# Attention scores from float32 keys and queries on eight 64x32 tiles, with three shared PSUM banks

## The chip, the cores and the metric

The kernel runs on one core of a Trainium2 chip. TensorE (PE) multiplies, VectorE (DVE), ScalarE (ACT) and GpSimd (POOL) work on elements, SyncE (SP) issues all transfers. SBUF has 128 partitions; PSUM, where PE writes, has eight banks of 512 float32 a partition. The metric is the device time of one execution in microseconds (us).

## The reference

Block-sparse attention with 4 batches, 8 heads, 768 positions and head size 64, followed by a feed-forward layer (FFN) with a rational function:

```python
    scores = scale * np.matmul(q, k.transpose(0, 1, 3, 2))      # scale = 1/8
    # mask: blocks of 32; a query block sees its neighbours (+-1), block 0,
    # block 23 and three sampled blocks; query blocks 0 and 23 see all
    scores = np.where(mask, scores, -1000000000.0)
    scores = scores - np.max(scores, axis=-1, keepdims=True)
    attn = np.exp(scores)
    attn = attn / (np.sum(attn, axis=-1, keepdims=True) + 1e-09)
    x = np.matmul(attn, v)                                      # then to [3072, 512]
    h = x @ w_in                                                # [3072, 2048]
    P = a[0] + a[1] * h + a[2] * h**2 + a[3] * h**3
    Q = 1.0 + np.abs(b[0]) * np.abs(h) + np.abs(b[1]) * h**2
    out = (P / (Q + 1e-06)) @ w_out                             # [3072, 512]
```

Inputs are float32, but for w_in and w_out (float64) and the numbers of the sampled blocks (integers).

## The kernel before

Attention is cut into *parts*: one query block (32 positions) of all eight heads against 8 key blocks (256 positions). An inner query block is one part (three neighbours, three sampled blocks, two edge blocks), blocks 0 and 23 take three parts each, so there are 28 parts a batch and 112 in all. The FFN is cut into 12 chunks of 256 tokens with 8 *units* each, 96 in all; a unit is 256 tokens by 256 of the 2048 inner columns.

*A part* runs so: scores on PE (`scores`, L872) into a PSUM tile `sp`, row maxima on DVE with the mask added (`maxima`, L882), the exponent on ACT (L897), four transposes on PE (L940) into `pt`, a copy to SBUF as `pT` on ACT (L147, inside the helper `times`), the product with the values on PE (L997) into `av`, and a division on DVE (L1024). Four query blocks together are transposed (L1034) into an `sp` tile and copied out as two float16 halves, `xh` on ACT and `xl` on DVE (L1046).

*The scores* use float16 pairs. A key or query tile is first scaled by a power of two, found from a bound: ACT sums absolute values (`bound`, L384), PE transposes the sums (L335), DVE takes the largest and makes the power (`scales`, L340 to L352). Then the tile is split into a high half (`high`, POOL) and a low half (`low`, DVE, L378), the halves are transposed on PE in eight matmuls (L660 keys, L733 queries), and copied to SBUF. The 128 partitions hold 64 elements high and 64 low. For queries a second copy `qc` with the halves exchanged is made by two DMAs (`swap`, L741); keys times `qa` and keys times `qc` add up to the full product. A part takes 16 matmuls of 128x32 tiles, four at a time in different columns, into one PSUM bank. The product of the two scales is undone in the exponent by a tensor `cq` (L721 to L727). For batches 1 to 3 the keys are loaded twice, once for the bound and once for the split (L580 and L532), and written to DRAM as `ks`, from where each part loads its 8 blocks into `kall` or `xkg`. For batch 0 they stay in `kall`, and POOL copies the sampled blocks to `kx` (L825).

*A unit* has two groups of 12 float16 matmuls (L1099 to L1101) into `ph`, five ACT and seven DVE instructions of 512 columns, and two groups of six matmuls (L1155 to L1157) into `acc`. The float64 weights arrive as 32 pieces through two load buffers `wl` and are decoded mainly by DVE (L434, L437, L440) during the first 250 us.

*The order* of all engines is made by the list planner `issue`: each `Op` has an engine, a price in ns, a priority, predecessors, and `Slot`s of `Ring`s, which stand for buffers. The planner takes the operation that can begin first by its prices. Where PE would wait before 80 us of planned time it puts in filling matmuls (`fill`, L159), which write to the accumulator's bank. PSUM rings: two banks `ph`, two `sp` (scores, transposed keys, queries, outputs and scales), one `pt`, and fixed banks for `av` and `acc`. Each engine then runs its list strictly in order.

## Time and profile before

| | us |
|---|---|
| median of 3 runs | 906.2 (902.2 to 910.01) |
| span of the profiled execution, first to last instruction | 897.2 |
| PE busy (share of the span) | 824.4 (92%) |
| DVE busy | 760.5 (85%) |
| ACT busy | 652.7 (73%) |
| POOL busy | 152.1 (17%) |
| chain that ended last: PE, DVE, DMA, ACT | 66%, 12%, 9%, 7% |

The span is the profiled execution's own time as far as the page gives it; 9.0 us lie between it and the median of the runs. Busy times overlap: an engine at 92% is the bound only where it is at 100%, so the busy times are read by stretch. PE's instructions are recorded with their latency: a record of 0.28 us follows the one before by 0.11. A share of the chain says which engine's work stood last at each moment.

### The profile page before, as it was taken

To read this page: it belongs to the slowest core of one execution; us is meant where nothing else is said; L and a number is where in the kernel's file an instruction comes from. 1 tells how busy PE (TensorE), PEld (TensorE's weight loads), DVE (VectorE), ACT (ScalarE), POOL (GpSimd) and SP (SyncE) were. 2 spreads that over 40 slices of the span, in tenths; PEclk is the share of its full clock that TensorE was granted. 3 is DMA by queue.
4 is the path that set the end of the run, shared out by engine and by line. 5 is a ranking of instruction groups with operands and counts; after the bars stand their busy time and mean duration, and the time that the engine had idled before them with its cause. 6 is when DMAs were issued, how large, how long until landed. Compare 5 with 4: busy or idle time off the path is not lost.

```text
span 897.2 us, 27426 instructions
## 1 busy us (share of the span) xinstructions
PE 824.4 (92%) x10310; PEld 640.1 (71%) x10310; DVE 760.5 (85%) x2042; ACT 652.7 (73%) x1380; POOL 152.1 (17%) x185
## 2 busy tenths in 40 slices
PE   6879868576899999989999999989999999999997
PEld 3446546465778787778888777778888877788885
DVE  4778978999998889879888788979888988788885
ACT  5587756677876878697778777788758687767563
POOL 2563743635310000110000000200000000000000
PEclk8989988698899999999999999999999999999999
DMA  8889686467966987688666986787756566740000
GB/s 222 186 186 233 177 175 165 113 166 202 237 162 168 239 227 172 176 207 196 165 150 184 250 204 157 168 208 197 155 148 176 145 160 169 172 110 25 1 24 24
DMA packets 238484, 148.04 MB, mean 165 GB/s; under 512 B 16016, under 2 KB 222736, under 8 KB 238352
## 3 DMA queue, kind: packets, MB, share of 16 engines
q1 hardware_dynamic: 238352, 146.29, 65.3%
q8 instruction: 82, 1.34, 0.7%
q14 instruction: 50, 0.41, 0.2%
HBM read 128.92 MB, written 11.01 MB: 156 GB/s over the span
## 4 chain that ended last, share of the span: by engine, by line
PE 66%; DVE 12%; DMA 9%; ACT 7%; SPq 3%; issue 2%; POOL 0%; ACTq 0%; POOLq 0%; DVEq 0%
PE acc L1155 8%; PE ph L1099 8%; PE acc L1157 8%; PE acc L1156 8%; PE ph L1101 7%; PE ph L1100 7%; PE av L997 6%; PE pt L940 5%; PE sp L872 4%; DMA wl<-in_moe_w_in_dram 2%; ACT pr L897 2%; PE acc L159 1%; DMA ld<-in_k_dram 1%; DVE pr L882 1%; DMA ks<-kt 1%
## 5 line engine op out<-in xcount | busy, mean ns | idle before, releaser
L1099 PE MATMUL ph<-xh,wi 128*128 128x256 f16 x768 | 210.9, 275 | 2.6 <-DVE tt L1116 2.6
L1101 PE MATMUL ph<-xh,wi 128*128 128x256 f16 x768 | 209.8, 273 | 0.0
L1100 PE MATMUL ph<-xl,wi 128*128 128x256 f16 x768 | 209.7, 273 | 0.0
L1155 PE MATMUL acc<-wo_h,gh 128*128 128x512 f32 x384 | 164.5, 428 | 5.0 <-ACT ld L147 4.9
L1157 PE MATMUL acc<-wo_h,gl 128*128 128x512 f32 x384 | 155.1, 404 | 7.3 <-DVE gl L1144 4.9
L897 ACT ACTIVATE pr<-pr,st,cq 128x256 f32<-128x256 f32 x224 | 132.3, 595 | 38.1 <-DVE st L908 35.1
L1156 PE MATMUL acc<-wo_l,gh 128*128 128x512 f32 x384 | 154.8, 403 | 1.6 <-POOL wo_l L451 1.6
L1106 ACT ACTIVATE sq<-ph,fc 128x512 f32<-128x512 f32 x96 | 65.6, 684 | 70.6 <-PE ph L1101 70.6
L151 POOL TENSOR_SCALAR hlq<-ldq,scq 128x512 f16<-128x512 f32 x24 | 24.8, 1032 | 452.1 <-DVE scq L352 235.4
L1123 DVE SCALAR_TENSOR_TENSOR ab<-sq,absb,ab 128x512 f32<-128x512 f32 x96 | 72.0, 750 | 34.4 <-ACT ab L1120 34.0
L1099 PEld LDWEIGHTS <-wi 128*128 128x128 f16 x768 | 75.2, 98 | 28.5 <-issue 16.2
L1157 PEld LDWEIGHTS acc<-wo_h,gl 128*128 128x128 f32 x384 | 74.1, 193 | 27.5 <-DVE gl L1144 7.6
L882 DVE CUSTOM_DVE_ANT_1 pr<-sp,bias 128x256 f32<-128x256 f32 x224 | 84.7, 418 | 6.9 <-PE sp L872 6.5
L1155 PEld LDWEIGHTS acc<-wo_h,gh 128*128 128x128 f32 x384 | 74.3, 194 | 21.4 <-ACT ld L147 5.2
L997 PE MATMUL av<-vg,pT 128*32 128x64 f32 x3584 | 74.4, 224 | 13.5 <-DMA vg<-in_v_dram 9.1
L1156 PEld LDWEIGHTS acc<-wo_l,gh 128*128 128x128 f32 x384 | 74.3, 193 | 14.8 <-POOL wo_l L451 2.1
L997 PEld LDWEIGHTS av<-vg,pT 128*32 128x32 f32 x3584 | 56.5, 111 | 39.6 <-issue 21.2
L940 PE MATMUL pt<-ident,pr 128*128 128x128 f32 x448 | 78.4, 296 | 5.0 <-ACT pr L897 2.3
L1100 PEld LDWEIGHTS <-wi 128*128 128x128 f16 x768 | 75.4, 98 | 10.2 <-issue 2.7
L1101 PEld LDWEIGHTS <-wi 128*128 128x128 f16 x768 | 75.2, 98 | 9.0 <-issue 0.2
L1134 DVE SCALAR_TENSOR_TENSOR gh<-tt,par,rr 128x512 fp32r<-128x512 f32 x96 | 73.9, 770 | 8.2 <-PE acc L1156 7.7
L147 ACT ACTIVATE pT<-pt 128x512 f32<-128x512 f32 x112 | 66.6, 594 | 18.1 <-PE pt L940 17.3
(141 smaller groups left out, 1697.1 us busy)
## 6 DMA issues: line engine op xcount, KB each, us to landing
vg<-in_v_dram SPq DMA_DIRECT2D x312, 64.0 KB, 3.4
vg<-in_v_dram SPq DMA_DIRECT2D x88, 192.0 KB, 3.9
vg<-in_v_dram SPq DMA_DIRECT2D x24, 512.0 KB, 4.7
kall<-ks SPq DMA_DIRECT2D x52, 192.0 KB, 3.6
kall<-ks SPq DMA_DIRECT2D x156, 64.0 KB, 2.2
ld<-in_k_dram SPq DMA_DIRECT2D x36, 256.0 KB, 4.8
wl<-in_moe_w_in_dram SPq DMA_DIRECT2D x32, 256.0 KB, 4.7
wl<-in_moe_w_out_dram SPq DMA_DIRECT2D x16, 512.0 KB, 4.6
```

The lines of the kernel that those rows point to most:

```text
L882: nc.vector.tensor_tensor_reduce(out=prs[x][:, g].rearrange("p (s r) -> p s r", r=BLK), in0=h["sp"][:, g].rearrange("p (s r) -> p s r", r= ...
L897: nc.scalar.activation(out=prs[x][:, g], in_=prs[x][:, g], func=AF.Exp, scale=Q["c"], bias=st[:, 6 + g:7 + g], accum_out=st[:, 8 + 2 * m + ...
L940: nc.tensor.transpose(pp[:, jj * P:(jj + 1) * P], cols, ident)
L997: nc.tensor.matmul(av[rows, g], pT[:, 2 * g + kt, rows] if plain else pT[:, 2 * g + kt, pa_, rows], vf[:, g * HG + h4, kt * D:(kt + 1) * D ...
L1099: nc.tensor.matmul(o, wh, xh[:, :, cc], start=(cc == 0), stop=False)
L1100: nc.tensor.matmul(o, wh, xl[:, :, cc], start=False, stop=False)
L1101: nc.tensor.matmul(o, wl, xh[:, :, cc], start=False, stop=(cc == NCC - 1))
L1123: nc.vector.scalar_tensor_tensor(out=d["ab"], in0=d["sq"], scalar=absb[:, 1:2], in1=d["ab"], op0=ALU.mult, op1=ALU.add)
L1134: nc.vector.scalar_tensor_tensor(out=d["gh"], in0=d["tt"], scalar=par[:, 0:1], in1=d["rr"], op0=ALU.add, op1=ALU.mult)
L1155: nc.tensor.matmul(acc[:, t], ghs, wo_h[:, f], start=(new and e == 0), stop=False)
L1156: nc.tensor.matmul(acc[:, t], ghs, wo_l[:, f], start=False, stop=False)
L1157: nc.tensor.matmul(acc[:, t], gls, wo_h[:, f], start=False, stop=(last and e == 1))
```

## The change

Keys and queries are no longer scaled, split or exchanged. A tile of 128 positions by eight heads is loaded once, with runs of 64 float32, four float32 transposes turn it (`turned`), two heads a transpose (head 2c in the upper 64 partitions, 2c + 1 in the lower), and one copy brings it to SBUF. A part's scores are eight float32 matmuls: 64 rows (one head) by 32 columns (32 queries) each, for near parts twice eight over 96 and 160 columns. The upper row half writes to one PSUM bank and the lower to another. The exponent takes the number 1/8 in place of `cq`. The rings `sp` and `pt` are joined to three banks, of which scores take two and any other user one; the planner learns to wait for several buffers of a ring. Fills end once the first accumulator is made. A w_in piece is loaded by one DMA in place of two, and the heads' order in it changes with `head`. The branch for values split in float16, which was not in use, is removed.

Instructions that the built programs hold, before and after: PE matmuls of scores 2144 and 1072 (in float32, loading their own weights), key and query transposes 384 and 192, scale transposes 36 and 8, fills 162 and 128; DVE low halves of keys and queries 48 and 0, key copies 6 and 3; ACT bounds of keys, queries and values 72 and 24, key copies 42 and 21; POOL high halves 48 and 0; DMAs 985 and 875. From the fifth unit on, the same number of parts, decoded weight pieces and units stand ahead of each other on PE and DVE to within one or two: when the 13th unit ends on DVE, 124 score reductions and 32 decoded pieces stand ahead of it in both. Ahead of the first unit PE has the values of 8 parts before, and of 11 now. The keys of batch 1 are turned among units 8 to 11 before, and now by the fifth.

DVE at the program's start, before (`hl` and `hlq` are key and query halves, `sc` and `scq` scales, `kall` the keys of batch 0):

```order
L724 TENSOR_SCALAR cq<-cq 128x1
L378 SCALAR_TENSOR_TENSOR hl<-tt,sc_214,hl 128x8x64 x2
L378 SCALAR_TENSOR_TENSOR hlq<-ldq,scq,hlq 128x8x64
L727 TENSOR_SCALAR cq<-cq 128x1
L149 COPY kall<-ph 128x4x8x16
L378 SCALAR_TENSOR_TENSOR hl<-ab,sc_214,hl 128x8x64
```

and now, from the end of the setup of the mask (`bias`) on:

```order
L321 TENSOR_SCALAR bias<-rr 128x24 x3
L150 COPY kall<-ph 128x4x4x32 x3
L620 TENSOR_REDUCE mx<-mx 128x1
L425 TENSOR_SCALAR wi<-wi 128x512
L771 ISA pr,st<-m_102,bias 128x256
```

Behind the setup DVE now has three key copies, the bound of the values and one step of a weight piece, and then the first part's maxima.

PE late in the program, before: the last products of a unit, a part's transposes into `pt`, and the next part's scores into one `sp` bank.

```order
L1155 MATMUL acc<-wo_h,gh 128x512
L1156 MATMUL acc<-wo_l,gh 128x512
L1157 MATMUL acc<-wo_h,gl 128x512
L940 MATMUL pt<-ident,pr 128x128 x4
L872 LDWEIGHTS qa
L872 MATMUL sp<-xkg_4398,qa 32x256
```

and now, at a like place (`m_101` to `m_103` are the three shared banks):

```order
L1015 MATMUL acc<-wo_h,gh 128x512
L1016 MATMUL acc<-wo_l,gh 128x512
L1017 MATMUL acc<-wo_h,gl 128x512
L828 MATMUL m_101<-ident,pr 128x128 x4
L761 MATMUL m_103<-kall,qt 32x256
L761 MATMUL m_102<-kall,qt 32x256
```

The transposes and the next scores stand as before, but together they now take all three banks, where the transposes had one of their own.

The diff, cut to its core:

```diff
-    ps_s = ctx.enter_context(tc.tile_pool(name="ps_s", bufs=2, space=PSUM))
-    ps_t = ctx.enter_context(tc.tile_pool(name="ps_t", bufs=1, space=PSUM))
+    ps_m = ctx.enter_context(tc.tile_pool(name="ps_m", bufs=1, space=PSUM))
...
+    banks = [ps_m.tile([P, 512], F32, name=f"m{i}") for i in range(3)]
...
-                    t = max([now[e], o.at[e]] + [s.ring.free[0][0] for s in o.takes])
+                    t = max([now[e], o.at[e]] + [r.free[m - 1][0] for r, m in o.rings.items()])
...
-                while f0 < fend:
+                while f0 < fend and not accs:
...
-    r_ph, r_sp, r_pt, r_acc = Ring([None] * 2), Ring([None] * 2), Ring([None]), Ring([None])
+    r_ph, r_sp, r_acc = Ring([None] * 2), Ring(range(3)), Ring([None])
...
-    kall = const.tile([P, NB, H, BLK], F16, name="kall")
+    kall = const.tile([P, NB, HG, BLK], F32, name="kall")
...
+    def turned(ld, pt):
+        for c in range(HG):
+            nc.tensor.transpose(pt[:, c * P:(c + 1) * P], ld[:, c * P:(c + 1) * P], ident)
...
+        def load():
+            d["ld"] = new()
+            nc.sync.dma_start(out=d["ld"].rearrange("p (h d) -> p h d", h=H), in_=k[b, :, t * P:(t + 1) * P].rearrange("h p d -> p h d"))
+        def transposes():
+            d["pt"] = ps_h.tile([P, 512], F32, name="ph") if first else banks[s_ps.buf]
+            turned(d["ld"], d["pt"])
+        def evac(eng):
+            if not half:
+                kts[b, t // 2] = kgs[t // 2] if first else p1.tile([P, KB, HG, BLK], F32, name="kt")
+            times(eng, kts[b, t // 2][:, half * TB:(half + 1) * TB].rearrange("p b c r -> p c b r"), d["pt"].rearrange("p (c b r) -> p c b r", c=HG, b=TB), 1.0)
...
-        o = Op(SC, 613, most, [o_ld], prio, uses=[s_ld])
-        o, sc = scales(lambda: d["mx"][:, 0:1], "scq", [o], prio, [s_sc])
-        h = Op(among("q", PO, po=671, ve=396, sc=613), 0, high, [o], prio, takes=[s_hl], uses=[s_ld, s_sc])
-        l = Op(VE, 663, low, [h], prio, uses=[s_ld, s_hl, s_sc])
-        d["oc"] = row(VE, [(70, factor), (69, factor2), (69, factor3)], [o, k_scale[b]], prio, takes=[d["cslot"]], uses=[s_sc])
-        x = Op(TE, 445, transposes, [l], prio, takes=[s_ps], uses=[s_hl])
-        x = Op(SC, 904, evac, [x], prio, takes=[d["slot"]], uses=[s_ps])
-        d["oq"] = Op(SY, [(650, 131072)] * 2, swap, [x], prio, uses=[d["slot"]])
+        x = Op(TE, 445, transposes, [o_ld], prio, takes=[s_ps, d["slot"]], uses=[s_ld])
+        d["oq"] = Op(SC, 520, evac, [x], prio, uses=[s_ps, d["slot"]])
...
-                    for g in range(2):
-                        for sl, kx in pieces:
-                            for jj, qx in enumerate((qa, qc)):
-                                for h4 in range(HG):
-                                    nc.tensor.matmul(spv[h4 * BLK:(h4 + 1) * BLK, g, sl], qx[:, g, h4, j % TB * BLK:(j % TB + 1) * BLK], kx[:, :, g * HG + h4],
-                                                     start=(jj == 0), stop=(jj == 1))
+                    for sl, kx in pieces:
+                        for h4 in range(HG):
+                            for g in range(2):
+                                rows = slice(g * D, (g + 1) * D)
+                                nc.tensor.matmul(h["sp"][g][h4 * BLK:(h4 + 1) * BLK, sl], Q["q"][rows, h4, j % TB * BLK:(j % TB + 1) * BLK], kx[rows, :, h4],
+                                                 start=True, stop=True)
...
-                        nc.scalar.activation(out=prs[x][:, g], in_=prs[x][:, g], func=AF.Exp, scale=Q["c"], bias=st[:, 6 + g:7 + g],
+                        nc.scalar.activation(out=prs[x][:, g], in_=prs[x][:, g], func=AF.Exp, scale=SCALE, bias=st[:, 6 + g:7 + g],
...
-                    h["pp"] = pp = ps_t.tile([P, 512], F32, name="pt")
+                    h["pp"] = pp = banks[s_pt.buf]
...
-            G["xt"] = ps_s.tile([P, 512], F32, name="sp")
+            G["xt"] = banks[s_ps.buf]
```

More of the change, by code (lines that the diff above doesn't have):

```diff
@@ L230, in issue @@
                 tick(t)
-                if now[e] < fend:
+                if now[e] < fend and not accs:
                     w = window
@@ L685, with tile_of @@
-    k_evac = {}
+            homes = [[(r_tt, "tt", p2), (r_ab, "ab", p2), (r_sq, "sq", p2)], [(r_pr, "pr", p3), (r_ld, "ld", p3)]]
+        def tile_of(w, j):
+            if not first:
+                slot = Slot(r_ld)
+                return slot, lambda: new_ld(slot)
+            ring, tag, pool = homes[w][j // (2 + w)]
+            return Slot(ring), lambda: pool.tile([P, 512], F32, name=tag, bufs={"tt": 3, "pr": 4}.get(tag))
+        before = None
+        for j in range(n):
+            before = keys(b, j, when(0, 1, j), before, *tile_of(0, j))
@@ new lines, in prep, with mx_tile, one, load @@
+        mx, los, before = {}, [], None
+        def mx_tile():
+            if 0 not in mx:
+                mx[0] = p4.tile([P, 8], F32, name="mx")
+            return mx[0]
+        for j in range(n):
+            def one(j, before):
+                prio = when(1, 0, j)
+                slot, new = tile_of(1, j)
+                d = {}
+                def load():
+                    d["ld"] = new()
+                    nc.sync.dma_start(out=d["ld"], in_=v[b].rearrange("h (a r) d -> (h a) (r d)", a=P // H)[:, j * 512:(j + 1) * 512])
+                def most():
+                    bound(d["ld"], mx_tile()[:, j:j + 1])
+                o = Op(SY, [(475, 262144)], load, (), prio - (1 if not first else 0), takes=[slot], behind=before)
+                los.append(Op(SC, 613, most, [o], prio, uses=[slot]))
+                return o
+            before = one(j, before)
@@ L751, in prep_q @@
-        x = Op(TE, 445, transposes, [l], prio, takes=[s_ps], uses=[s_hl])
-        x = Op(SC, 904, evac, [x], prio, takes=[d["slot"]], uses=[s_ps])
-        d["oq"] = Op(SY, [(650, 131072)] * 2, swap, [x], prio, uses=[d["slot"]])
+            d["q"] = p2.tile([P, HG, P], F32, name="qt")
+            nc.scalar.activation(out=d["q"].rearrange("p c r -> p (c r)"), in_=d["pt"], func=AF.Copy)
+        o_ld = Op(SY, [(650, 262144 // len(runs(t)))] * len(runs(t)), load, (), prio - 1, takes=[s_ld], behind=before)
@@ L1001, in two @@
-                ol = chain["vg"] = Op(SY, price, load, [o_setup] + v_done[b],
-                                      prio[m] - 0.72, takes=[s_vg], uses=[] if plain else [s_scr[b]], behind=chain.get("vg"))
-                dv = [ol]
-                o = chain["tr"] = Op(TE, 435, turn, [oexp[m]], p, behind=chain.get("tr"), takes=[s_pt], uses=[s_pr])
-                l = Op(among("t", SC, sc=478, ve=598), 0, whole if plain else high, [o], p, takes=[s_pT], uses=[s_pt])
-                if not plain:
-                    l = Op(VE, 602, low, [l], p, uses=[s_pt, s_pT])
@@ L1008, in two @@
-                o = chain["av"] = Op(TE, 560 if plain else 470, values, [l] + dv, p + 0.1, behind=chain.get("av"), takes=[s_av] if m == 0 else [], uses=[s_pT, s_vg] + ([] if m == 0 else [s_av]))
+                                nc.tensor.matmul(av[rows, g], pT[:, 2 * g + kt, rows], vf[:, head(h4, g), kt * D:(kt + 1) * D],
+                                                 start=(kt == 0 and (n == 1 or (m == 0 and g == 0))), stop=(m == n - 1 and kt == 1), skip_group_check=n > 1)
+                ol = chain["vg"] = Op(SY, price, load, [o_setup],
+                                      prio[m] - 0.72, takes=[s_vg], behind=chain.get("vg"))
@@ L1009, in two @@
+                dv = [ol]
+                o = chain["tr"] = Op(TE, 435, turn, [oexp[m]], p, behind=chain.get("tr"), takes=[s_pt, s_pT], uses=[s_pr])
+                l = Op(among("t", SC, sc=478, ve=598), 0, whole, [o], p, uses=[s_pt, s_pT])
+                o = chain["av"] = Op(TE, 560, values, [l] + dv, p + 0.1, behind=chain.get("av"), takes=[s_av] if m == 0 else [], uses=[s_pT, s_vg] + ([] if m == 0 else [s_av]))
                 oval.append(o)
@@ L1242 @@
     prep(0, when(0))
[L1243 removed]
+    chain["edges"] = Op(PO, 1400, edges, k_evac[0], -40, uses=s_kall)
     weights()
```

338 lines of the change are left out of this document (86 added, 252 removed).

## The prediction

> **What bounds the kernel now.** I read the page first, then busy time by stretch (columns: stretch, its length, then busy us with instructions in brackets for PE, weight loads, DVE, ACT and POOL, granted clock, DMA share, GB/s), cut where the work changes its kind.
>
> ```profile
> span 897.2 us, 27426 instructions
> 0.00:75.00 75.00, 59.37 (x838) 32.13 (x839) 51.20 (x193) 48.55 (x118) 33.62 (x64) 0.91 0.84 198
> 75.00:303.00 228.00, 183.49 (x2433) 138.58 (x2432) 208.35 (x526) 165.87 (x358) 90.90 (x95) 0.92 0.72 182
> 303.00:805.00 502.00, 494.71 (x6410) 398.72 (x6409) 428.89 (x1212) 385.34 (x815) 27.62 (x27) 1.00 0.72 178
> 805.00:897.00 92.00, 86.82 (x636) 70.66 (x633) 72.08 (x116) 52.98 (x92) 0.00 (x0) 0.99 0.07 24
> ```
>
> The same stretches for one line, L1099, which every FFN unit runs eight times, tell how many units each holds; the same for L872 (16 a part once all parts are far ones) and L335.
>
> ```profile
> 75.00:303.00 228.00, 44.29 (x161) 15.86 (x161) 0.92 0.72 182
> 303.00:805.00 502.00, 137.56 (x503) 49.13 (x502) 1.00 0.72 178
> 303.00:805.00 502.00, 45.42 (x1200) 26.73 (x1200) 1.00 0.72 178
> 303.00:805.00 502.00, 5.53 (x19) 2.66 (x19) 1.00 0.72 178
> ```
>
> So there are four stages. Until 75 us no unit runs: DVE is busy 68% of the time, and the stage is a chain of latencies. From 75 to 303 us there are 161/8 = 20 units, 11.4 us each, with DVE at 208.35/228 = 91% and PE at 80%: DVE sets the pace. From 303 to 805 us there are 63 units at 8.0 us and 1200/16 = 75 parts, and PE is idle 502 - 494.71 = 7.3 us in all: PE sets it, and less work on DVE or ACT is worth next to nothing. Behind 805 us only units are left. A saving is therefore worth its DVE time in the second stage and its PE time in the third.
>
> **The start.** The chain of waits, in order of time (start, us, what), and the first and last start of L872:
>
> ```profile
> 5.83 5.64 DMA sq<-in_k_dram
> ...
> 18.52 0.46 PE ph L660 x8
> ...
> 23.57 0.76 ACT kall L147
> L872 PE MATMUL sp<-kall,qa x736: 202/273/421, 32.7 to 804.0; 128*32 128x256 f16 x140, 128*32 128x96 f16 x44
> L1099 PE MATMUL ph<-xh,wi x768: 269/273/421, 75.2 to 879.9; 128*128 128x256 f16 x192
> ```
>
> The last keys land at 5.83 + 5.64 = 11.5 us, but all six tiles must then pass bound, scale and two splits before the last copy out ends at 24.3. Without scale and splits, the last tile needs four transposes (0.6, fence below) and one copy (0.75): 12.8 us, 11.5 earlier. The first query tile loses its scale, its splits and two swap DMAs, so the first scores (32.7 us) can come by about as much earlier. The first unit (75.2 us) also needs the first four pieces of w_in, whose loads and decoding stay. Bounds 0 (the pieces decide) and -14 (11.5 and a swap); I take -12, as the scores are 42 us ahead of the unit and the pieces share DVE and ACT with what goes.
>
> **The second stage.** Groups of DVE instructions between 75 and 303 us (count | busy us, mean ns | idle before):
>
> ```profile
> L908 DVE TENSOR_SCALAR st<-st,cq 128x2 f32<-128x2 f32 x23 | 9.1, 400 | 0.0
> L919 DVE TENSOR_SCALAR st<-st 128x2 f32<-128x2 f32 x23 | 6.7, 289 | 3.7 <-ACT pr L897 3.7
> L378 DVE SCALAR_TENSOR_TENSOR hl<-ld,sc,hl 128x512 f16<-128x512 f32 x6 | 5.6, 939 | 1.3 <-POOL hl L151 1.3
> L378 DVE SCALAR_TENSOR_TENSOR hlq<-ldq,scq,hlq 128x512 f16<-128x512 f32 x5 | 4.9, 979 | 0.4 <-POOL hlq L151 0.4
> L721 DVE SCALAR_TENSOR_TENSOR cq<-scq,sc 128x1 f32<-128x1 f32 x5 | 1.5, 296 | 0.0
> L340 DVE TENSOR_REDUCE scq<-sp 128x1 f32<-128x128 f32 x5 | 1.4, 278 | 0.0
> L343 DVE TENSOR_SCALAR scq<-scq 128x1 f32<-128x1 f32 x5 | 0.7, 147 | 0.0
> ...
> L352 DVE TENSOR_SCALAR scq<-scq 128x1 int32<-128x1 int32 x5 | 0.7, 143 | 0.0
> L340 DVE TENSOR_REDUCE sc<-sp 128x1 f32<-128x128 f32 x2 | 0.6, 284 | 0.0
> ```
>
> Gone: low halves of six key and five query tiles 5.6 + 4.9; query scale and factors 1.5 + 1.4 + 6 rows of 0.7; one of the two scales of batch 1, about 1.0 with its small steps; and L908, whose factor becomes a number as in L919, 23 x (400 - 289) ns = 2.6. Sum 21.2 us. The work between two units is otherwise the same (the counts stand with the change), so at 91% the stage shrinks by 21.2/0.91 = 23. ACT and POOL lose work too and do not take the bound. What is late next is the decoding of weights behind its two load buffers, and PE. Bounds 0 and -23; nearest is the row at 91%: -22.
>
> **The third stage: PE.** The timeline of PE in the third stage (start, us, operation):
>
> ```profile
> 464.24 0.63 PE L940 MATMUL pt<-ident,pr 128*128 128x128 f32 x4
> 464.80 0.29 PE L872 MATMUL sp<-kall,qa 128*32 128x256 f16 x4
> 464.92 0.28 PE L872 MATMUL sp<-kall,qc 128*32 128x256 f16 x4
> 465.03 0.28 PE L872 MATMUL sp<-kall,qa 128*32 128x256 f16 x4
> 465.14 0.28 PE L872 MATMUL sp<-kall,qc 128*32 128x256 f16 x4
> 465.35 0.28 PE L1099 MATMUL ph<-xh,wi 128*128 128x256 f16 x1
> ...
> 466.56 0.27 PE L1101 MATMUL ph<-xh,wi 128*128 128x256 f16 x1
> 466.77 0.65 PE L997 MATMUL av<-vg,pT 128*32 128x64 f32 x32
> 467.35 0.28 PE L1099 MATMUL ph<-xh,wi 128*128 128x256 f16 x1
> ```
>
> *Scores.* Before: four column tiles run at once, in four rounds 0.11 us apart, 0.55 us with the way out. After: eight matmuls, in float32. The values (av) are float32 already: 16 matmuls of the program leave 32 records, so each is made in two passes; eight rounds of four take 467.35 - 466.77 = 0.58 us, 0.48 without the 0.10 that switching costs (466.56 + 0.11 to 466.77). That is 0.060 us for 64 columns, 0.24 for 256. If all eight tiles run at once, a part needs two rounds, 0.48 instead of 0.44: +0.04 x 75 = +3 us. Bounds: two rounds at the float16 rate, 0.22 (-16 us), and at the gross 0.58/8 for 64 columns, 0.58 (+10 us). Two halves in turn is rival A. *Transposes.* Four float32 ones (0.56 from 464.24) replace eight float16 ones (0.46 at 18.52): 0.1 x 27 tiles is at most 3 us, and the trace has both with their switches, so 0. *Scale transposes (L335).* 15 of the 19 are of queries, 0.29 us busy each; pipelined beside others less: -2 to -4, I take -3. *Idle time.* Of the 7.3 us some stands at the key tiles of batches 2 and 3: 0 to -7, I take -3.
>
> *Banks.* A part now takes two of three banks, and transposed weights, queries, keys and outputs draw on the same three. What holds a bank:
>
> ```profile
> L882 DVE CUSTOM_DVE_ANT_1 pr<-sp,bias 128x256 f32<-128x256 f32 x224 | 84.7, 418 | 6.9 <-PE sp L872 6.5
> L147 ACT ACTIVATE pT<-pt 128x512 f32<-128x512 f32 x112 | 66.6, 594 | 18.1 <-PE pt L940 17.3
> ```
>
> Two reductions are 0.84 us and an evacuation 0.59, both behind one or two other instructions of 0.7. In the changed order, counted with the durations above, 13 of 275 takings of a bank in this stage have under 2.2 us of other PE work since its last writer. 0 to +13 us; I take +3. Behind a waiting score matmul stand all units on PE's queue, so this counts in full. *Short runs.* Keys and queries now land in runs of 256 B; here DMA is at 0.72 and nothing waits for it: 0, as long as that cover stands.
>
> *Priced at nothing.* SP issues 110 DMAs fewer (swaps, second key loads, w_in pieces in one DMA instead of two); in the third stage PE waits for none of them, so the cover is PE's own work. ACT loses bounds and the larger half of its key and query copies; it is 385.34/502 = 77% busy there, under PE. The fills now end with the first accumulator; they only stand where PE waits, and the pace of the second stage is DVE's. If the clock falls without them, it costs something only where PE is the bound, and there it is at 1.00 without fills.
>
> **Sum:** -12 - 22 + 3 - 3 - 3 + 3 = -34, a span of 863. The median of the runs, 906.2, is 9.0 above the profiled span; with as much around it, 872 us.
>
> **Rivals.**
> A, the other side: the upper and the lower half of the array take turns. Then four rounds of 0.24 us: +0.48 us a part, 75 x 0.48 = 36 in the third stage and, since PE has room there, half of 37 x 0.48 for the other parts (224 reductions, two a part, make 112): +45, a span of 908, 917 us. It decides from 34/(75 + 37/2) = 0.36 us a part. Nothing in this trace has row halves; for it speaks only that, against it that column tiles start together. The Trainium skill, TensorEngine Tiling (Array Packing), Tiling Modes, lists 64x32 as eight independent tiles that load and multiply in parallel; by it A falls, and no run here shows it yet.
> B: the second stage is held by the loads and the decoding of weight pieces, and what DVE saves turns into idle time. Then -22 is 0: 885, 894 us. Against it stands DVE at 91%; for it, that such loads lie on the chain of waits:
>
> ```profile
> 130.56 5.86 DMA wl<-in_moe_w_in_dram
> ```
>
> C: short runs cost as much as those of 512 B.
>
> ```profile
> q1 hardware_dynamic: 238352, 146.29, 65.3%
> ```
>
> A packet takes 0.653 x 897.2 x 16/238352 = 0.039 us of an engine. Six key tiles of batch 0 have 512 more each: 3072 x 0.039/16 = 7.5 us later keys: 870, 879 us. The Trainium skill, DMA: Bandwidth & Descriptors, Specifications, says that transfers under 512 B miss line rate because the engine reads, modifies and writes; by it the sum is C's. No run here shows it yet.
> D: with POOL's splits gone, DVE's other instructions get shorter as well. The stage's 20 units have 7 long ones each; 0.08 us less is 11 us: 852, 861 us.
>
> **How the numbers follow.** My forecast 0.48 (its own range 860 to 884), B 0.18, A 0.12, D 0.12, C 0.10. The predicted time is the forecast's, 872. From 850 to 903 it leaves out A and the lower part of D, under 0.2. One per cent (897 to 915) is about what a measurement can tell: faster is the forecast, D, C and over half of B, 0.81; the same 0.10 (the rest of B, a mild A); slower 0.09.
>
> **What would show it.** Right: first scores near 21 us and first unit near 63; 20 units after that in about 206 us with DVE still near 90%; in the third stage 8.0 us a unit, PE idle under 7 us; two rounds of eight scores 0.24 us apart. Wrong: rounds of four with the halves in turn (A); DVE under 85% in the second stage at an unchanged pace (B); keys landing after 18 us (C); PE waiting at the scores for a reduction or a copy out of a bank, by more than 0.3 us a part.

## The result, and the profile after

| | before | after |
|---|---|---|
| median of 4 runs, us | 906.7 (902.2 to 910.01) | 869.9 (868.9 to 871.65) |
| ratio after/before, 95% interval | | 0.960 (0.957 to 0.963) |
| span of the profiled execution, us | 897.2 | 868.1 |

The kernel became 4.0% faster. The profiled execution of the kernel after took 869.87 us with a span of 868.1, so only 1.8 us lie around its span. The spans differ by 29.1 us, the medians by 36.8; the experiments come to that.

From the page after, the span and the busy time of the engines:

```profile
span 868.1 us, 26226 instructions
PE 812.3 (94%) x10056; PEld 617.4 (71%) x10056; DVE 699.2 (81%) x1773; ACT 578.8 (67%) x1263; POOL 98.7 (11%) x139
```

Busy time by stretch after, cut where the stages change (stretch, length, then busy us with instructions for PE, weight loads, DVE, ACT and POOL, granted clock, DMA share, GB/s):

```profile
0.00:72.00 72.00, 56.26 (x947) 33.45 (x948) 40.78 (x170) 39.09 (x103) 20.02 (x57) 0.95 0.87 199
72.00:280.00 208.00, 174.82 (x2197) 128.83 (x2196) 188.79 (x440) 142.28 (x313) 78.65 (x82) 0.94 0.67 179
280.00:777.00 497.00, 495.56 (x6278) 385.90 (x6276) 398.42 (x1050) 345.04 (x760) 0.00 (x0) 1.00 0.65 168
777.00:868.00 91.00, 85.69 (x640) 69.25 (x638) 71.24 (x115) 52.36 (x91) 0.00 (x0) 0.99 0.06 20
```

The second and third stretch for the first matmul of a unit alone (L959 now, L1099 before), which again tell the units:

```profile
72.00:280.00 208.00, 44.11 (x162) 15.84 (x162) 0.94 0.67 179
280.00:777.00 497.00, 137.88 (x503) 49.16 (x502) 1.00 0.65 168
```

The first unit starts at 72.0 us, 3.2 earlier than before. Twenty units take 208 us where they took 228, with DVE still at 188.79/208 = 91%. In the third stage PE is idle for 497 - 495.56 = 1.4 us, where it was 7.3.

In every kernel of this study 35 parts stand ahead of the 21st unit and 77 behind it, so the start of that unit is the best place to cut. Before, it is at 302.8 us:

```profile
0.00:302.80 302.80, 242.66 (x3267) 170.54 (x3267) 259.35 (x718) 214.22 (x474) 124.52 (x158) 0.92 0.75 186
302.80:897.20 594.40, 581.73 (x7047) 469.55 (x7043) 501.17 (x1325) 438.52 (x907) 27.62 (x27) 1.00 0.62 154
```

After, it is at 279.6:

```profile
0.00:279.60 279.60, 230.69 (x3138) 161.93 (x3138) 229.35 (x608) 180.96 (x413) 98.67 (x139) 0.95 0.72 184
279.60:868.10 588.50, 581.65 (x6926) 455.50 (x6918) 469.88 (x1165) 397.81 (x851) 0.00 (x0) 1.00 0.56 145
```

Ahead of the cut DVE has 259.35 - 229.35 = 30.0 us less to do, but is idle for 50.3 us in place of 43.5: a gain of 23.2. Behind the cut PE has the same work to 0.1 us, and its idle time falls from 12.7 to 6.9 us: a gain of 5.9. Together 29.1. These are two single executions; a second one of each kernel (before_again and after_again below) gives gains of 27.2 and 8.5 us.

What PE waited for in the third stage before (us in total, times, longest):

```profile
PE sp L872 <- ACT kt L147: 4.7, 3, 2.0
PE av L997 <- ACT pT L147: 1.3, 2, 1.0
```

and after, where these are all the waits of PE in it:

```profile
PE m L522 <- DMA ldq<-in_q_dram: 1.2, 1, 1.2
PE av L863 <- ACT pT L148: 0.2, 1, 0.2
```

In the third stage no score matmul waits for a bank any more. A part's scores on PE's timeline after (start, us, operation):

```profile
448.33 0.65 PE L863 MATMUL av<-vg,pT 128*32 128x64 f32 x32
448.91 0.66 PE L761 MATMUL m<-kall,qt 64*32 64x256 f32 x16
449.51 0.28 PE L959 MATMUL ph<-xh,wi 128*128 128x256 f16 x1
```

They hold PE for 449.51 - 448.91 = 0.60 us, where 0.55 was read before. Their sixteen records are two for each of eight matmuls; eight records begin within 0.05 us, and the second eight 0.24 us behind them.

### The profile page after: what moved, and what is told of

It reads as the page before. It is cut to its first block, busy times and chain, and to the rows that moved or that the text cites. A ratio compares the mean times of both kernels' runs of the same rounds, so it can differ in the third digit from the quotient of the medians.

```text
span 868.1 us, 26226 instructions
## 1 busy us (share of the span) xinstructions
PE 812.3 (94%) x10056; PEld 617.4 (71%) x10056; DVE 699.2 (81%) x1773; ACT 578.8 (67%) x1263; POOL 98.7 (11%) x139
## 4 chain that ended last, share of the span: by engine, by line
PE 72%; DVE 12%; DMA 8%; SPq 4%; ACT 2%; issue 2%; ACTq 0%; DVEq 0%
PE acc L1015 9%; PE ph L959 9%; PE acc L1017 9%; PE acc L1016 9%; PE ph L960 8%; PE ph L961 8%; PE av L863 6%; PE m L761 6%; PE m L828 5%; DMA wl<-in_moe_w_out_dram 2%; PE m L522 2%; DMA ld<-in_k_dram 2%; DMA wl<-in_moe_w_in_dram 2%; DMA ld<-in_v_dram 1%; DMA ldq<-in_q_dram 1%
## 5 line engine op out<-in xcount | busy, mean ns | idle before, releaser
L959 PE MATMUL ph<-xh,wi 128*128 128x256 f16 x768 | 210.5, 274 | 1.1 <-DVE tt L976 1.1
L1015 PE MATMUL acc<-wo_h,gh 128*128 128x512 f32 x384 | 162.5, 423 | 0.6 <-ACT ld L148 0.5
L1016 PE MATMUL acc<-wo_l,gh 128*128 128x512 f32 x384 | 152.7, 398 | 1.2 <-POOL wo_l L442 1.2
L786 ACT ACTIVATE pr<-pr,st 128x256 f32<-128x256 f32 x224 | 111.3, 500 | 33.5 <-DVE st L797 33.4
L959 PEld LDWEIGHTS <-wi 128*128 128x128 f16 x768 | 75.2, 98 | 43.0 <-issue 24.0
L771 DVE CUSTOM_DVE_ANT_1 pr<-m,bias 128x256 f32<-128x256 f32 x224 | 85.6, 419 | 12.9 <-PE m L761 12.3
L148 ACT ACTIVATE pT<-m 128x512 f32<-128x512 f32 x112 | 65.9, 594 | 29.3 <-PE m L828 28.7
L828 PEld LDWEIGHTS m<-ident,pr 128*128 128x128 f32 x448 | 67.8, 206 | 20.8 <-ACT pr L786 7.1
L828 PE MATMUL m<-ident,pr 128*128 128x128 f32 x448 | 75.3, 292 | 7.7 <-ACT pr L786 3.3
L960 PEld LDWEIGHTS <-wi 128*128 128x128 f16 x768 | 75.2, 98 | 7.8 <-issue 0.4
L863 PE MATMUL av<-vg,pT 128*32 128x64 f32 x3584 | 72.4, 224 | 3.7 <-DMA vg<-in_v_dram 2.8
```

Source lines behind the costliest of these rows:

```text
L771: nc.vector.tensor_tensor_reduce(out=prs[x][:, g].rearrange("p (s r) -> p s r", r=BLK), in0=h["sp"][g], in1=add.rearrange("p (s o) -> p s ...
L786: nc.scalar.activation(out=prs[x][:, g], in_=prs[x][:, g], func=AF.Exp, scale=SCALE, bias=st[:, 6 + g:7 + g], accum_out=st[:, 8 + 2 * m + ...
L828: nc.tensor.transpose(pp[:, jj * P:(jj + 1) * P], pr[:, g, kt:NS * BLK:2], ident)
L863: nc.tensor.matmul(av[rows, g], pT[:, 2 * g + kt, rows], vf[:, head(h4, g), kt * D:(kt + 1) * D], start=(kt == 0 and (n == 1 or (m == 0 an ...
L959: nc.tensor.matmul(o, wh, xh[:, :, cc], start=(cc == 0), stop=False)
L960: nc.tensor.matmul(o, wh, xl[:, :, cc], start=False, stop=False)
```

## The experiments

Each kernel was timed beside the kernel before on the same chip: before_again to one_half together, then k55 to runs512, then, on another chip, after_again to wl4. In the table the ratio is that to the kernel before; "first" and "21st" are the starts of the first and the 21st unit, "rest" is the time from there to the end of the span, all in us of the profiled execution.

| kernel | median us | ratio (95%) | span | first | 21st | rest |
|---|---|---|---|---|---|---|
| before | 906.7 | | 897.2 | 75.2 | 302.8 | 594.4 |
| after | 869.9 | 0.960 (0.957-0.963) | 868.1 | 72.0 | 279.6 | 588.5 |
| before_again | 903.8 | 1.000 (0.998-1.003) | 901.4 | 75.9 | 303.7 | 597.7 |
| dve_early | 877.5 | 0.971 (0.968-0.974) | 875.8 | 71.0 | 285.9 | 589.9 |
| dve_late | 870.4 | 0.963 (0.959-0.966) | 869.3 | 71.9 | 279.1 | 590.2 |
| one_half | 901.8 | 0.998 (0.996-1.000) | 900.4 | 70.9 | 282.2 | 618.2 |
| k55 | 870.6 | 0.965 (0.961-0.969) | 868.2 | 68.1 | 278.3 | 589.9 |
| wl3 | 862.8 | 0.955 (0.950-0.959) | 862.7 | 67.9 | 272.8 | 589.9 |
| banks21 | 880.0 | 0.975 (0.971-0.979) | 877.2 | 74.9 | 285.8 | 591.4 |
| runs512 | 864.9 | 0.958 (0.954-0.962) | 863.5 | 68.4 | 275.5 | 588.0 |
| after_again | 868.4 | 0.960 (0.957-0.964) | 865.7 | 70.8 | 276.5 | 589.2 |
| scale_t | 871.7 | 0.963 (0.959-0.966) | 870.9 | 72.6 | 280.8 | 590.1 |
| act_late | 874.8 | 0.967 (0.963-0.970) | 873.3 | 71.5 | 279.9 | 593.4 |
| wl4 | 869.2 | 0.961 (0.957-0.964) | 865.8 | 62.7 | 275.5 | 590.3 |

The kernel after itself varies by 3.1 us at the 21st unit (279.6 and 276.5) and by 0.7 in the rest, the kernel before by 0.9 and 3.3, which is the measure for the differences below. One source of this shows in the clock: over the first 21 us the granted clock was 0.92 in the profiles of the kernel after and of k55, where the first scores came at 20.8 us, and 1.00 in those of the other changed kernels, where with the same loads they came at 19.1 or 19.2.

### before_again: the kernel before, unchanged

> The kernel before, unchanged. Its profiled execution had a span of 897.2 us and the median of its runs was 906.7; the kernel after has 868.1 and 869.9, so 1.8 us lie around its span. Theory: as much lies around the span of the kernel before, its profiled execution was simply one of its quickest, and the others have spans of 900 to 908 us with a lower granted clock than 0.970. Rival: about 9 us that the span does not hold belong to the kernel before, so that its spans stay near 897 while its times are 902 to 910.

In each of its 10 runs, and of the 19 runs of the kernel before beside it, the time is 1.7 to 1.9 us above the span; the spans go from 896.8 to 906.3 us. The theory holds, but for the clock: 0.961 to 0.975, and the times do not follow it closely. The profiled execution of the kernel before, by that 897.2 + 1.8 = 899.0 us, was one of its shortest, 7.7 below its median of 906.7. This one is 0.9 us later at the 21st unit and 3.3 longer behind it. PE's waits in the third stage differ too: its score matmuls wait 2.4 us for key copies in place of 4.7, and once for a load of values, for which they did not wait in the first profile.

```profile
PE sp L872 <- DMA vg<-in_v_dram: 3.0, 1, 3.0
```

### dve_early and dve_late: the same VectorE work in two stages

```diff
+    spare = const.tile([P, 512], F16, name="spare")
...
             nc.vector.tensor_tensor(out=d["gl"], in0=d["tt"], in1=d["rr"], op=ALU.mult)
+            if 0 <= k0 < 20:
+                twice = ident.rearrange("p (o c) -> p o c", o=1).broadcast_to([P, 4, P])
+                nc.vector.scalar_tensor_tensor(out=spare.rearrange("p (o c) -> p o c", o=4), in0=twice, scalar=0.5, in1=twice, op0=ALU.mult, op1=ALU.add)
```

In dve_late the condition is `30 <= k0 < 50`.

> After, with one more VectorE instruction of 128x512 in each of the first 20 units, reading a constant and writing a tile that nobody reads. Such instructions take 0.75 us (L983 760 ns), so 20 x 0.75 = 15 us of work. Theory (VectorE sets the pace of the second stage, which is where the 20 us were gained): 15 to 16 us slower, 885 to 886 us, the third stage unchanged. Rival (the 20 us came from ACT, POOL or the transfers that went away, and VectorE has room): less than 4 us slower.

> After, with the same 20 added VectorE instructions in units 30 to 49, which run in the third stage. Theory (PE sets the pace there, VectorE is 80% busy): 0 to 2 us slower, 870 to 872 us. Rival (VectorE's work counts in every stage): 15 us slower, 885 us.

In dve_late the rest is 590.2 us, where it lies between 588.0 and 590.3 in the kernels whose work and banks there are those of the kernel after: the 11.2 us by which VectorE's busy time grew behind the 21st unit are free in the third stage. In dve_early 18 of the 20 stand ahead of the 21st unit (626 instructions of DVE where 608 stood):

```profile
0.00:285.90 285.90, 234.23 (x3138) 163.92 (x3138) 238.05 (x626) 180.49 (x413) 99.19 (x139) 0.93 0.72 180
285.90:875.80 589.90, 581.69 (x6926) 455.50 (x6918) 471.17 (x1167) 397.49 (x851) 0.00 (x0) 1.00 0.57 145
```

DVE's busy time ahead of that unit grew by 8.7 us against the kernel after (10.2 against after_again, which has 227.84), and the unit came 6.3 us (9.4) later; the median is 7.1 above that of dve_late on the same chip. So a microsecond of VectorE's busy time added there costs 0.7 to 0.9 us. The expectation of 15 us was too high mainly in the work: two instructions fell behind the stage, and one takes 0.69 us by its record, not 0.75, and overlaps its neighbours, so that the busy time grew by 9 to 10 and not by 15. In the kernel after DVE is never idle between the 9th and the 13th unit (174.30 to 216.20), but 18% of the time between the first and the fifth:

```profile
72.00:148.10 76.10, 54.76 (x719) 37.91 (x718) 62.66 (x150) 50.77 (x120) 38.00 (x43) 0.87 0.77 213
148.10:174.30 26.20, 23.78 (x271) 18.60 (x271) 25.39 (x52) 20.67 (x44) 15.28 (x19) 1.00 0.55 146
174.30:216.20 41.90, 35.10 (x524) 25.84 (x522) 41.90 (x101) 27.90 (x62) 19.62 (x17) 0.96 0.59 165
216.20:249.60 33.40, 30.79 (x331) 22.64 (x324) 32.98 (x77) 22.69 (x47) 5.75 (x6) 1.00 0.67 168
249.60:279.60 30.00, 30.00 (x368) 23.49 (x360) 25.64 (x63) 19.85 (x43) 0.00 (x0) 1.00 0.63 156
```

Over the last four of the twenty units it is PE that is busy throughout, and DVE no longer sets the pace.

### one_half: the price of row halves in turn

```diff
-                                rows = slice(g * D, (g + 1) * D)
+                                rows = slice(0, D)
                                 nc.tensor.matmul(h["sp"][g][h4 * BLK:(h4 + 1) * BLK, sl], ...
```

> After, with all score matmuls reading the upper 64 rows, so that the scores of the odd heads are left out and those of the even heads are made twice, into the two banks as before. Theory (in the kernel after both row halves work at once, and here they cannot): each part has four rounds of 0.24 us in place of two, 0.48 x 74 = 36 us in the third stage and up to 9 us for the 38 parts before it: 906 to 915 us. Rival 1 (the halves take turns in the kernel after as well, or PE has room in the third stage): within 3 us of 870. Rival 2 (column tiles of one half are delayed too): over 920 us.

On PE's timeline a part's scores now read:

```profile
450.92 1.09 PE L761 MATMUL m<-kall,qt 64*32 64x256 f32 x16
451.94 0.28 PE L959 MATMUL ph<-xh,wi 128*128 128x256 f16 x1
```

They hold PE for 451.94 - 450.92 = 1.02 us in place of 0.60. The records begin in four rounds of four, 0.24, 0.22 and 0.22 us apart. The rest is 618.2 - 588.5 = 29.7 us longer, 0.39 for each of 77 parts, and the median comes back to that of the kernel before. The theory holds in kind; the price is a little under the 36 us expected, in part since a later round costs 0.22 and not 0.24. So in the kernel after the two row halves work at once, and that is worth about as much as the whole change gained. The Trainium skill, TensorEngine Tiling (Array Packing), Tiling Modes, lists 64x32 as eight independent tiles; the trace agrees, for float32 too, which the page does not treat.

### k55: keys of batch 1 later

```diff
-        A = [8.9, 8.52] if b == 1 else [11.69, 8.81]
+        A = [8.9, 5.5] if b == 1 else [11.69, 8.81]
```

> After, with the keys of batch 1 loaded and turned about three units later (the number 8.52 of their due time becomes 5.5), so that on PE's queue four of their transposes fewer stand ahead of the first unit. In the kernel after, these wait for a load until 71.4 us, and the first unit begins at 72.0; the last decoded piece of its weights comes from POOL at 70.0. Theory (the weight pieces hold the first unit): it begins at 70 to 71 us, and the time is 0 to 2 us less: 868 to 870. Rival (the key load on SP's queue holds it): it begins at 65 us or earlier and the time falls by 4 to 7 us: 863 to 866.

The first unit began at 68.1 us, 3.9 earlier, between the theory and the rival; the last low half of its pieces ended at 68.4 in place of 70.0. The time did not change. The fifth unit begins at 126.9 in place of 148.1, the ninth at 170.7 in place of 174.3, the 13th at 218.6 in place of 216.2, the 21st at 278.3 in place of 279.6. So an earlier first unit was worth nothing here: all that is won is lost again by the 13th unit.

### wl3 and wl4: more load buffers for weights

```diff
-    r_wl, r_dw, r_kx, r_sums = Ring([None] * 2), ...
+    r_wl, r_dw, r_kx, r_sums = Ring([None] * 3), ...
...
-                d["ld"] = early.tile([P, 2 * WC], I32, name="wl", bufs=2)
+                d["ld"] = early.tile([P, 2 * WC], I32, name="wl", bufs=3)
```

In wl4 both numbers are 4.

> After, with three load buffers for weight pieces in place of two; the planner then puts the fourth piece of w_in ahead of the values of three parts on SP's queue, and 8 parts instead of 11 ahead of the first unit on PE's. Theory (the first unit was held by its fourth piece, which SP issued at 48.5 us in the kernel after, 42.9 before, although its buffer was free from 38.7): the first unit begins at 60 to 65 us; with VectorE 82% busy in the first four units about half of the 7 to 12 us stays to the end: 862 to 867 us. Rival 1 (VectorE's remaining work sets the end of the second stage wherever the first unit begins): first unit earlier, time within 2 us of 870. Rival 2 (the transfers get in each other's way, values land later): slower than 872.

> After, with four load buffers for weight pieces (two in the kernel after, three in wl3, which took 862.8 us). Theory (with three buffers the pieces are no longer held by SP's queue, and VectorE's work sets the rest): within 3 us of wl3, 860 to 866. Rival (loads still decide until 200 us): another 4 to 6 us less, 856 to 859.

SP's timeline of the kernel after shows what the fourth piece stood behind: after the second and third (the two issues from 29.32) come the values (`vg`) of five parts.

```profile
29.32 1.85 SPq L416 DMA_DIRECT2D wl<-in_moe_w_in_dram  x2
...
45.76 0.38 SPq L841 DMA_DIRECT2D vg<-in_v_dram  x1
47.03 1.32 SPq L847 DMA_DIRECT2D vg<-in_v_dram  x3
48.46 0.84 SPq L416 DMA_DIRECT2D wl<-in_moe_w_in_dram  x2
```

In the kernel before, where a piece takes two DMAs, four issues from 29.78 are the second and third piece, and the fourth goes out at 39.10, as soon as its buffer is free; what goes out at 42.9, the figure in the expectation, is the fifth.

```profile
29.78 2.42 SPq L425 DMA_DIRECT2D wl<-in_moe_w_in_dram  x4
39.10 4.88 SPq L425 DMA_DIRECT2D wl<-in_moe_w_in_dram  x4
```

In the kernel after DVE took the last reading of the buffer that this load waits for at 38.05 to 38.72 us:

```profile
38.05 0.67 DVE L431 SCALAR_TENSOR_TENSOR wi<-wl,wi 128x512 int32<-128x512 int32 x1
```

With three buffers SP issues the fourth piece at 30.4, the first unit starts at 67.9 with 8 parts ahead of it, and the 21st unit at 272.8, 6.8 earlier than in the kernel after and 3.7 than in after_again:

```profile
67.90:140.30 72.40, 56.01 (x770) 40.04 (x769) 70.58 (x161) 49.78 (x117) 45.27 (x50) 0.85 0.91 230
```

In the first four units DVE is busy for 70.58/72.40 = 97%, where it was 82%. Ahead of the 21st unit it runs the same 608 instructions as in the kernel after; their busy time is even 5 us longer (234.52 in place of 229.35), but DVE is idle for 38.3 us in place of 50.3: the gain is idle time alone. The four runs took 859.8 to 864.5 us; the eight of the kernel after 867.5 to 871.7. The ratios differ by 0.005 with intervals that overlap, so wl3 is about 5 us faster than the kernel after, near the edge of what was measured. The first unit did not come as early as 60 to 65 us, as the last low half of its pieces was done only at 66.9; the time is as the theory said. The planner also changed the order (8 parts ahead in place of 11), so the earlier load alone was not tried.

The expectation for wl4 failed both ways. Its first unit starts at 62.7 us, ten earlier than after, but the fifth at 147.5; the 21st starts at 275.5 and the time is that of the kernel after. The planner makes another order for each number of buffers, and why this one loses by the fifth unit what it had won was not settled.

### banks21: banks divided as before

```diff
-    r_ph, r_sp, r_acc = Ring([None] * 2), Ring(range(3)), Ring([None])
+    r_ph, r_sp, r_acc = Ring([None] * 2), Ring(range(2)), Ring([None])
+    r_pt = Ring([2])
...
-                s_pt, s_pT, s_vg = Slot(r_sp), Slot(r_pT), Slot(r_vg)
+                s_pt, s_pT, s_vg = Slot(r_pt), Slot(r_pT), Slot(r_vg)
```

> After, with the banks divided as before: one for the transposes of the exponents alone, two for scores, keys, queries and outputs, of which a part's scores take both. Theory (the third stage lost its 5.9 us of idle time because fewer and shorter copies hold a bank, sharing matters little): 0 to 3 us slower, 870 to 873 us. Rival (sharing three banks is what took PE's idle time away and makes two-bank scores possible at all): 6 to 20 us slower, with PE waiting in the third stage at the scores or the transposes for VectorE's maxima and ACT's copies.

It is 9.4 us slower than k55 beside it, of which 7.5 come ahead of the 21st unit and 1.5 behind. The rival had the size, but not the place: in the third stage PE waits only once (2.0 us, for an output copy), as the theory would have it. Ahead of the 21st unit the score matmuls (L762 here) wait for what last held their banks, the maxima and the copy of `xl`, both DVE's:

```profile
PE m L762 <- DVE st L772: 4.8, 4, 2.4
PE m L762 <- DVE xl L909: 3.7, 1, 3.7
```

In the kernel after they wait about as long ahead of that unit, though:

```profile
PE m L761 <- DVE st L771: 4.4, 2, 4.1
PE m L761 <- ACT kt L148: 3.3, 1, 3.3
```

PE's idle time ahead of the 21st unit is the same in both, 285.8 - 237.06 = 48.7 us and 279.6 - 230.69 = 48.9. So dividing the banks cost time in the first two stages, but these waits do not show how. The planner makes another order here too; against the kernel after the loss is already there at the fifth unit (158.9 us in place of 148.1), and its cause stays open.

### runs512: the length of the runs

```diff
-            nc.sync.dma_start(out=d["ld"].rearrange("p (h d) -> p h d", h=H), in_=k[b, :, t * P:(t + 1) * P].rearrange("h p d -> p h d"))
+            nc.sync.dma_start(out=d["ld"].rearrange("p (h n) -> p h n", h=4), in_=k[b, t % 2 * 4:t % 2 * 4 + 4, t // 2 * 2 * P:(t // 2 + 1) * 2 * P].rearrange("h (p s) d -> p h (s d)", s=2))
```

The loads of queries are changed in the same way.

> After, with key and query tiles loaded in runs of 512 bytes (four heads of 256 positions in place of eight heads of 128); as many bytes a tile, but the keys and queries then stand in another order, so that the attention comes out of wrong pairs. Theory (short runs cost nothing): within 2 us of 870, first scores still near 20.8 us. Rival (a short run costs as much as a long one): the keys of batch 0 land up to 7 us earlier, first scores at 15 to 18 us, and the time falls by 3 to 7 us.

The first scores come at 17.7 us, the first unit at 68.4, and the 21st at 275.5. By the median this is 5.0 us under the kernel after (5.7 under k55 on the same chip), by the ratios 2; the intervals overlap. Of the 3.1 us by which the first scores come earlier than in the first profile of the kernel after, 1.4 are left against after_again (19.1 us), whose granted clock in the first 21 us was 1.00, as here, and not 0.92. SP's timeline tells where these come from. In the kernel after:

```profile
2.13 1.06 SPq L542 DMA_DIRECT2D tt<-in_k_dram  x2
3.24 2.79 SPq L542 DMA_DIRECT2D ab<-in_k_dram  x2
6.07 2.29 SPq L542 DMA_DIRECT2D sq<-in_k_dram  x2
8.41 1.32 SPq L639 DMA_DIRECT2D ldq<-in_q_dram  x1
```

with runs of 512 bytes:

```profile
3.16 1.06 SPq L542 DMA_DIRECT2D ab<-in_k_dram  x2
4.26 2.21 SPq L542 DMA_DIRECT2D sq<-in_k_dram  x2
6.51 1.09 SPq L639 DMA_DIRECT2D ldq<-in_q_dram  x1
```

With short runs SP is held longer by the issues themselves, and the first query tile goes out 1.9 us later (after_again has the same figures to 0.02 us). The rival's time came about, but not its reason: the keys go out, and land, up to 2 us earlier and not 7, and what the later loads gain was not separated. From issue to landing a key tile takes as long either way (4.6 to 5.2 us, and 4.8 to 5.7). The Trainium skill, DMA: Bandwidth & Descriptors, Specifications, puts the loss under 512 B into the DMA engine's read, modify and write; these runs agree that short runs cost something, and show it in the issue.

### after_again: the kernel after, unchanged

> The kernel after, unchanged, on the same chip as the three kernels below, for comparison with them. Both theories: 868 to 872 us, and a ratio to the kernel before of 0.957 to 0.966, as measured at first (0.960).

Measured as at first: 868.4 us (867.5 to 870.65) and a ratio of 0.960.

### scale_t: the factor as a tile again

```diff
-                        nc.scalar.activation(out=prs[x][:, g], in_=prs[x][:, g], func=AF.Exp, scale=SCALE, bias=st[:, 6 + g:7 + g],
+                        nc.scalar.activation(out=prs[x][:, g], in_=prs[x][:, g], func=AF.Exp, scale=eighth[:, 0:1], bias=st[:, 6 + g:7 + g],
...
+    eighth = const.tile([P, 2], F32, name="eighth")
...
+        nc.vector.memset(eighth[:, 0:1], SCALE)
+        nc.vector.memset(eighth[:, 1:2], -SCALE)
...
-            nc.vector.tensor_scalar(out=d["st"][:, 6:8], in0=d["st"][:, 0:2], scalar1=-SCALE, ...
+            nc.vector.tensor_scalar(out=d["st"][:, 6:8], in0=d["st"][:, 0:2], scalar1=eighth[:, 1:2], ...
```

> After, with the factor 1/8 of the exponents (L786) and of the negative maxima (L797) read from a tile of 128x1 as before the change, in place of a number; nothing is left out. Theory: the exponents take 595 ns again in place of 500, which is 224 x 0.095 = 21 us of ACT's time, and the negative maxima about 280 in place of 170 ns, some 4 us of VectorE's time before 280 us; VectorE's time there was worth 0.7 to 1 us each, ACT's nothing, so 1 to 4 us slower than the kernel after. Rival 1 (ACT's 21 us count in the second stage, where exponents and decoding share ACT): 5 to 10 us slower. Rival 2 (the longer exponents of before came from the work beside them and not from the tile): the exponents stay at 500 ns and the time within 1 us.

The groups of exponents (count | busy us, mean ns | idle before), after:

```profile
L786 ACT ACTIVATE pr<-pr,st 128x256 f32<-128x256 f32 x224 | 111.3, 500 | 33.5 <-DVE st L797 33.4
```

and with the tile:

```profile
L789 ACT ACTIVATE pr<-pr,st,eighth 128x256 f32<-128x256 f32 x224 | 131.9, 592 | 36.2 <-DVE st L800 36.1
```

So the tile costs an exponent 92 ns. The median is 3.4 us above that of after_again on the same chip. In the profiles the 21st unit comes 4.3 us later than in after_again (1.2 than in the first profile of the kernel after); ahead of it DVE has 2.5 us and ACT 6.2 us more to do. That is inside the theory; how much of it is ACT's was not separated.

### act_late: ACT's queue in the third stage

```diff
         def evac(eng):
...
+            if b >= 2:
+                for _ in range(3):
+                    nc.scalar.activation(out=scrap.rearrange("p (o c) -> p o c", o=4), in_=ident.rearrange("p (o c) -> p o c", o=1).broadcast_to([P, 4, P]), func=AF.Abs)
             times(eng, kts[b, t // 2]..., d["pt"]..., 1.0)
```

> After, with three more ACT instructions of 128x512 (a constant to a tile that nobody reads) ahead of each of the 12 key copies of batches 2 and 3 in the third stage: 36 x 0.6 = 22 us of ACT's time, about what the bounds and the second half of the copies took there before. Theory (PE's 5.9 us less of idle time came from shorter queues on ACT in front of the key copies that hold a bank; before, the scores waited 4.7 us for them): PE waits again in the third stage, at scores or transposes for the key copies, and the kernel is 2 to 6 us slower. Rival (the idle time went because of the shared banks or fewer transfers): no new wait on PE, within 1 us.

The median is 6.4 us above that of after_again; in the profiles 4.2 us stand behind the 21st unit, which is inside the theory. But PE waits little where the theory said. What its matmuls wait for in the third stage is exponents and the copies of their transposes, which stand behind the added work on ACT's queue:

```profile
PE m L831 <- ACT pr L789: 1.3, 2, 1.1
PE av L866 <- ACT pT L148: 1.1, 2, 0.6
PEld m L764 <- ACT kt L148: 1.0, 2, 0.5
```

The last line is the only sign of the key copies: the weight loads of two score matmuls wait for them. PE's idle time behind the 21st unit is 9.1 us, where after_again has 7.5; the other 2.6 of the 4.2 us stand in PE's busy time (584.27 in place of 581.70), and no run tells why.

So some 20 us of ACT's time in lumps of 2 us cost about 4 us there, although with them ACT is busy for only 365.54/502 = 73% of the stage, while what dve_late added to DVE in pieces of 0.7 us cost next to nothing.

## Why the prediction came near: its steps one by one

The forecast was 872 us, the measured median 869.9; the forecast saving was 34 us, and the medians lie 36.8 apart (36.5 beside after_again). The 9.0 us that the sum puts around the span were not work around it: 1.8 lie there, and the other 7.2 are what a short execution of the kernel before fell below the median of its runs. The spans of the two first profiles therefore lie only 29.1 apart. By stages, in two executions of each kernel (us; the second are before_again and after_again):

| | forecast | first | second |
|---|---|---|---|
| to the first unit | -12 | -3.2 | -5.1 |
| the next twenty units | -22 | -20.0 | -22.1 |
| from the 21st unit on | 0 | -5.9 | -8.5 |
| sum | -34 | -29.1 | -35.7 |

So the reason for the largest term held, and the sum came out in part by luck: too much for the start and too little for the third stage nearly cancel.

**The start, -12: the step that failed.** The first scores came where forecast (20.8 and 19.1 us, "near 21"), the first unit at 72.0 instead of 63. What failed is the overlap, "as the scores are 42 us ahead of the unit and the pieces share DVE and ACT with what goes", and the row for the pieces, whose bound of 0 took them for the limit before the change as well. Before, they were not: the last low half of the first four pieces was done at 64.8 us, and the unit waited for the second half of its attention outputs (`xl`), done at 74.2. Now the outputs are done at 56.1 and the pieces at 70.0. In order, two lines from before and two from after:

```profile
63.62 1.21 POOL L498 TENSOR_TENSOR wi<-dw,wi 128x512 f16<-128x512 f32 x1
73.40 0.75 DVE L1046 SCALAR_TENSOR_TENSOR xl<-sp,xscale,xh 128x512 f16<-128x512 f32 x1 [0.55 <-ACT xh L147]
55.38 0.74 DVE L908 SCALAR_TENSOR_TENSOR xl<-m,xscale,xh 128x512 f16<-128x512 f32 x1
68.61 1.34 POOL L489 TENSOR_TENSOR wi<-dw,wi 128x512 f16<-128x512 f32 x1 [1.16 <-ACT wi L148]
```

With the pieces as early as before, some 10 us were to be had. They came 5.2 us later: the fourth piece was issued at 48.5 us in place of 39.1, although its buffer was free at 38.7, because the planner had put the values of five parts ahead of it on SP's queue. The order had shown 11 parts ahead of the first unit instead of 8, and what stands ahead of the prediction says so; the prediction did not price what their loads do to SP. How much of the 5.2 us that late issue makes is open: in wl3 the piece goes out 18 us earlier, but the last low half is done only 3 us earlier, at 66.9; wl3 gains 3.7 to 6.8 us at the 21st unit. k55 shows a second error: the start and the second stage do not add up, since a first unit that comes 3.9 us earlier leaves the 21st where it was.

**The second stage, -22: right.** 227.6 us for twenty units became 207.6, -20.0, with DVE at 91% as before. The reason holds in kind: dve_early makes it slower with VectorE's work alone, dve_late with the same work does not. In size, 207.95 - 188.57 = 19.4 us less of DVE's busy time brought 20.0, and a microsecond added to the kernel after cost 0.7 to 0.9; if one taken away is worth as much, 14 to 17 of the 20 us are VectorE's. No run put the removed work itself back. The rest may come from what ACT and POOL lost ahead of the 21st unit (33 and 26 us of work), which was not tried on its own, but for the exponents in scale_t. That work is not all there is to it shows in wl3, which is faster with the same DVE instructions and less of DVE's idle time.

**The third stage, 0: measured -5.9 and -8.5.** PE's work was forecast well as a sum: +3 for the scores and -3 for the scale transposes, and its busy time behind the 21st unit changed by 0.1 us (by 1.9 between the second executions). The two terms of waiting were mis-sized. Idle time fell by 5.8 us and not by 3, as the 4.7 us at key copies went whole; act_late shows that ACT's queue can make such idle time, though mostly at other instructions, so why it went is argued and not shown. The banks, forecast at +3, cost nothing: PE waits for none in the third stage. banks21 shows that they matter ahead of it, where the prediction gave them no price.

**What was priced at nothing.** Fewer DMAs: no run tells of them alone. Short runs, at 0: 2 to 6 us, of which 1.4 are seen at the first scores. Fewer fills: the granted clock did not fall without them, it was 0.95 ahead of the 21st unit where it had been 0.92 (0.94 and 0.90 in the second executions); what the higher clock is worth there was not tried.

**The rivals.** A falls: eight records within 0.05 us; its price, 45 us forecast, was 32 in one_half. B falls as it was put: DVE stayed at 91% and the pace changed; but loads of weight pieces do hold the start. C is right in sign and too large: 7.5 us forecast. D falls, as DVE's long instructions did not get shorter: 760 ns now for that of `ab`, 750 before. The group before and after:

```profile
L1123 DVE SCALAR_TENSOR_TENSOR ab<-sq,absb,ab 128x512 f32<-128x512 f32 x96 | 72.0, 750 | 34.4 <-ACT ab L1120 34.0
L983 DVE SCALAR_TENSOR_TENSOR ab<-sq,absb,ab 128x512 f32<-128x512 f32 x96 | 73.0, 760 | 40.6 <-ACT ab L980 40.4
```

## What to carry to other kernels

Cut two profiles at a point that has the same work ahead of it, and count there the work and the idle time of the engine that bounds each side; a stage's first event is no such point, and moving it earlier may be worth nothing. Take each profile twice before a few microseconds of a stage are explained. When a planner or a pool decides the order, look at what has come to stand ahead of each load on the issuing queue, and not only at the engines. Compare a profiled execution with the median of the runs through the spans of all runs, before a difference is taken for work that the span does not hold.

## What the runs showed of the hardware

- Eight 64x32 tiles in float32 work at once: two rounds of 256 columns, 0.24 us apart. With all of them in one row half there are four rounds, 0.24, 0.22 and 0.22 us apart.
- An exponent of 128x256 takes 500 ns with a number as its scale and 592 to 595 with a 128x1 tile. The Trainium skill, ScalarE: Activation LUTs, What ACT_TABLE_LOAD costs, gives about 93 ns for each such operand; the trace agrees with 92 and 95.
- A load of 256 KB in runs of 256 bytes holds SP's queue for 0.4 to 1.8 us at the start of the program. In runs of 512 bytes the two `ab` loads hold it for 1.06 us in place of 2.79, the six key loads together for 4.3 in place of 6.1.
- The time of a run was 1.7 to 2.0 us above its span in all runs, but for those of wl4 (2.1), while the span of one and the same kernel before moved by 10 us (896.1 to 906.3).
- With the granted clock at 0.92 in place of 1.00 over the first 21 us, the same program had its first scores 1.7 us later (20.8 and 19.1 us in the two profiles of the kernel after).
